# Block rows of the mask moved between a DMA, VectorE and GpSimd in a fused attention and gated MLP kernel

## The chip, the cores and the metric

The kernel runs on one core of a Trainium2 chip. The metric is the device time of one execution in microseconds (us). TensorE (PE, weight loads PEld), VectorE (DVE), ScalarE (ACT), GpSimd (POOL) and SyncE (SP, which here only issues DMAs) each work through a queue of their own in order and wait for one another by semaphores.

## The reference

Block-sparse attention (4 batches, 8 heads, 768 positions, head dimension 64), then a gated MLP with a product over positions. Inputs and output are float32.

```python
def _attn_ref(q, k, v, sampled_blocks):            # B, H, S, D = 4, 8, 768, 64
    scores = np.matmul(q, k.transpose(0, 1, 3, 2)) / np.sqrt(D)
    # blocks of 32: neighbours, first and last block row and column,
    # and 3 sampled key blocks for each query block
    scores = np.where(mask, scores, -1e9)
    attn = np.exp(scores - scores.max(-1, keepdims=True))
    attn = attn / (attn.sum(-1, keepdims=True) + 1e-09)
    return np.matmul(attn, v)

def _moe_ref(x, w_in, w_spatial, b_spatial, w_out):  # x: 4 x 768 x 512
    h = np.maximum(x @ w_in, 0.0)                     # 1024 wide
    u, v = h[..., :512], h[..., 512:]
    v_n = (v - mean(v)) / np.sqrt(var(v) + 1e-06)
    v_s = np.einsum('ts,bsd->btd', w_spatial, v_n) + b_spatial[None, :, None]
    return (u * v_s) @ w_out
```

## The kernel before

**The operand of the scores.** One tile `kq` of 88 partitions holds, for each of the 8 heads of a batch, the keys in its first 768 columns (`K_`) and the queries in the next 768. Partitions 0 to 63 hold the head dimension. Partitions 64 to 87 (`MR`) hold the mask, one partition for each of the 24 key blocks: a one-hot of the block in the key columns, and in the query columns what the mask adds to the scores of this block. One matmul over 88 rows so gives masked scores. The mask is the same for every head: it is made once, in head 0, and copied to the other heads. These copies are the block rows, and `rows` (L243) makes one on an engine, `rows_dma` (L250) by a DMA on the SP queue. Block rows are written once; later batches overwrite partitions 0 to 63 alone.

**Slots.** The program is a loop of slots (L845). Each slot puts the score matmuls of one piece into TensorE's queue, one exponential into ScalarE's queue, then the products with V of an earlier piece, then the work that tables assign to the slot, in this order: `at`, the MLP steps (`run_queue`), `late`, `post`. The order within each engine's queue is thus fixed when the program is built; the times follow from the waits.

Batch 0 takes the slots 0 to 35. Its queries come in three thirds of 256 columns (`qcols(0)`, `qcols(1)`, `qcols(2)`), and a unit (`UNITS`, L427) is one third for one pair of heads, three slots long:

| slots | what | block rows needed |
|---|---|---|
| 0 to 5 | first third (and more) of heads 0 and 1 | heads 0, 1 |
| 6 to 14 | first third of pairs 1, 2, 3 (pair 3, heads 6 and 7, in 12 to 14) | `K_` and `qcols(0)` of heads 2 to 7 |
| 15 to 23 | second third of pairs 1 to 3 | `qcols(1)` of heads 2 to 7 |
| 24 to 35 | third third of pairs 0 to 3 | `qcols(2)` of all heads |

From slot 36 on a head takes six slots, and the other three batches follow; their loads, casts, transposes (`tr_dma`) and copies into `kq` (`split`) are set by slot numbers (L816 to L829). The MLP products of batch 0 begin in slot 15 and run between the scores.

**Where block rows are made before the change.** VectorE copies most, by the list `ROWS` (L739): entries are slot, first head, last head, columns. `qcols(1)` of heads 2 and 3 and `qcols(2)` of heads 2 to 7 come by two DMAs (L332, L353).

**What stands around them.** In VectorE's queue: `tr_first` (L384) copies a pair's keys and first third from PSUM into `kq` in slots 4, 7 and 10 (pair 3 in 10); `normalize` (reciprocal L474, product L475 into `xn`); copies of transposed `xn` into `xt`; evictions of MLP products (`ts`, L186), the statistics of `v` (L619, L620) and its normalization, also L186, which waits for `rstd` from GpSimd (L625). In GpSimd's queue: float32 to bfloat16 casts of q, k, v (L137), of `w_in` (L234), of `w_spatial` (L556), in the order of the program. In the SP queue: the loads of batch 0 and of `w_in`, then `b_col` (L364), the loads of pair 4 (k, q, v), six loads `ws_f` of `w_spatial` and the transposing DMA of pair 4. A load waits for the buffer that it writes and for the DMA that was issued eight before it on this queue.

Of the kernel before, what the change touches and what calls it, by code (L numbers as in the profile page):

```python
# [26 lines left out]
def kernel(  # L27
# [16 lines left out]
    nc = tc.nc  # L44

    B, H, S, D = q.shape
    BLK = 32
    NB = S // BLK
# [16 lines left out]
    TW = TC * 128  # L65
# [17 lines left out]
    kq = const.tile([KR, H, 2 * S], BF16, name="kq")  # L83
    NVV = 6
    vv = [const.tile([128, 2, NCH, VS], BF16, name=f"vv{s}") for s in range(NVV)]
    MR = slice(D, KR)
    K_, Q_ = slice(0, S), slice(S, 2 * S)

    def qcols(t0, n=1):
        return slice(S + t0 * TW, S + (t0 + n) * TW)  # L90
# [24 lines left out]
    def nat0_view():  # L115
        return nat[0].rearrange("p c h d -> p (c h d)").rearrange("p (h x) -> p h x", h=2)

    def cast(p, nm, eng, hs=BOTH, cs=ALLC):
        if nm == "v":
            dst = vv[p % NVV][:, hs, cs, 0:D]  # L120
        else:
            if p not in nat:
                nat[p] = work.tile([128, 2 * NCH, 2, D], BF16, tag="nat", bufs=4, name="nat")
            c0 = 0 if nm == "k" else NCH
            dst = nat[p][:, c0 + cs.start:c0 + cs.stop].rearrange("p c h d -> p h c d")[:, hs]
        src = st[nm, p].rearrange("p h (c d) -> p h c d", d=D)[:, hs, cs]
        if p == 0 and nm != "v":
            dst = nat0_view()[:, hs, (c0 + cs.start) * D:(c0 + cs.stop) * D]
            if cs is not C45:
                dst = dst[:, 0].rearrange("p (i t d) -> p t i d", t=2, d=D)  # L130
                src = src[:, 0].rearrange("p (t i) d -> p t i d", t=2)
            else:
                dst = dst.rearrange("p h (c d) -> p h c d", d=D)
        if eng is nc.scalar:
            nc.scalar.activation(out=dst, in_=src, func=AF.Copy)
        else:
            eng.tensor_copy(out=dst, in_=src)  # L137
# [77 lines left out]
    PL, DV = nc.gpsimd, nc.vector  # L215
# [14 lines left out]
    def w_in_load(u, g):  # L230
        w_load((u, g), moe_w_in[g * 128:(g + 1) * 128, 0 if u else DH:DH if u else DFF])

    def w_in_cast(u, g, eng):
        eng.tensor_copy(out=w_in_t[:, g, 0 if u else DH:DH if u else DFF], in_=wst.pop((u, g)))  # L234
# [8 lines left out]
    def rows(hs, cs, eng=nc.vector):  # L243
        src = kq[MR, 0:1, cs].to_broadcast([NB, hs.stop - hs.start, cs.stop - cs.start])
        if eng is nc.scalar:
            nc.scalar.activation(out=kq[MR, hs, cs], in_=src, func=AF.Copy)
        else:
            eng.tensor_copy(out=kq[MR, hs, cs], in_=src)  # L248

    def rows_dma(t, h1):  # L250
        nc.sync.dma_start(out=kq[MR, 2:h1, qcols(t)],
                          in_=kq[MR, 0:1, qcols(t)].to_broadcast([NB, h1 - 2, TW]))

    cast(0, "k", nc.scalar, H0, C03)
    cast(0, "q", PL, H0, C03)
    rows(H1, K_)
# [72 lines left out]
    m1()  # L329
    m2()  # L330
    rows(H1, qcols(0, 3))
    rows_dma(1, 4)  # L332
    w_in_load(0, 1)
    load(2, "q", cs=C25)
    w_in_load(0, 2)
# [9 lines left out]
    cast(1, "v", PL)  # L345
    cast(2, "v", PL)
    cast(1, "q", PL, cs=C25)
    w_in_cast(0, 0, PL)
    w_in_load(1, 3)
    cast(3, "v", PL)  # L350
    w_in_cast(0, 1, PL)
    w_in_load(1, 2)
    rows_dma(2, H)  # L353
    cast(2, "q", PL, cs=C25)
    w_in_cast(0, 2, PL)
    w_in_cast(0, 3, PL)
# [376 lines left out]
    def when(slot, *fns):  # L733
        at.setdefault(slot, []).extend(fns)

    def c(f, *a, **kw):
        return lambda: f(*a, **kw)

    ROWS = [(1, 2, 4, qcols(0)), (1, 2, 3, K_), (3, 3, 4, K_), (4, 4, 6, qcols(0)), (6, 4, 6, K_), (7, 6, 8, qcols(0)), (9, 6, 8, K_), (15, 4, 8, qcols(1))]  # L739
    when(0, second)  # L740
    when(1, third)
    when(2, lambda: filler(FILL3, psum.tile([128, 512], FP32, tag=moe_tag(), bufs=1, name="wps")))
# [3 lines left out]
    when(10, c(tr_first, 3))  # L746
    for sl, h0, h1, cs in ROWS:
        when(sl, c(rows, slice(h0, h1), cs))
# [146 lines left out]
```

## Time and profile before

| | us |
|---|---|
| median of 3 runs | 211.81 |
| lowest, highest | 211.39, 212.13 |
| profiled execution, its own time | 212.83 |
| its span, first to last instruction | 209.9 |
| granted TensorE clock, mean | 0.997 |

The profile is of one execution. A line of a timeline gives start, duration, engine, source line, operation, output<-input and, in brackets, idle time of the engine before it and what ended it. SPq and PEq are sequencers; an SPq row is the issue of a DMA, not its transfer. A line of the chain of waits gives start, duration and the instruction that the end depended on. The engine groups of the page, the windows, the chain and the timelines that matter are shown in the prediction.

### The profile page before, as it was taken

To read this page: it belongs to the slowest core of one execution; us is meant where nothing else is said; L and a number is where in the kernel's file an instruction comes from. 1 tells how busy PE (TensorE), PEld (TensorE's weight loads), DVE (VectorE), ACT (ScalarE), POOL (GpSimd) and SP (SyncE) were. 2 spreads that over 40 slices of the span, in tenths; PEclk is the share of its full clock that TensorE was granted. 3 is DMA by queue.
4 is the path that set the end of the run, shared out by engine and by line. 5 is a ranking of instruction groups with operands and counts; after the bars stand their busy time and mean duration, and the time that the engine had idled before them with its cause. 6 is when DMAs were issued, how large, how long until landed. Compare 5 with 4: busy or idle time off the path is not lost.

```text
span 209.9 us, 5241 instructions
## 1 busy us (share of the span) xinstructions
PE 200.5 (96%) x2107; PEld 127.1 (61%) x2141; DVE 133.7 (64%) x294; ACT 167.7 (80%) x222; POOL 69.7 (33%) x108
## 2 busy tenths in 40 slices
PE   7898999899999999999999999999999999999992
PEld 6597878666666666665565556665565556544441
DVE  7899675988864545484986464375884443476551
ACT  5898999899989989989998888979999787266021
POOL 6685759675564123033065050131020000012000
PEclk9999999999999999999999999999999999999998
DMA  5999899999999999999955597795101225520275
GB/s 146 343 363 324 279 352 253 272 232 249 275 350 241 257 185 285 242 293 336 209 194 112 131 246 167 202 269 159 37 3 35 52 53 118 196 78 0 50 191 211
DMA packets 64356, 41.93 MB, mean 200 GB/s; under 512 B 45196, under 2 KB 59084, under 8 KB 64332
## 3 DMA queue, kind: packets, MB, share of 16 engines
q1 hardware_dynamic: 63756, 41.01, 75.7%
q10 hardware_dynamic: 576, 0.59, 0.8%
q8 instruction: 16, 0.26, 0.6%
q14 instruction: 8, 0.07, 0.1%
HBM read 24.38 MB, written 6.29 MB: 146 GB/s over the span
## 4 chain that ended last, share of the span: by engine, by line
PE 78%; DVE 6%; DMA 5%; POOL 3%; SPq 2%; issue 2%; ACT 1%; ACTq 0%; DVEq 0%
PE ps_moe L584 29%; PE ps L459 22%; PE ps_av L510 12%; PE ps_t L584 8%; PE ps_sc L584 4%; DMA ws_f<-in_moe_w_spatial_dram 3%; POOL ws_b L556 2%; DVE kq L218 2%; DMA st_q<-in_q_dram 2%; DVE vn L186 2%; SPq L109 2%; PE ps_av L492 1%; PE ps L446 1%; DVE kq L248 1%; PE ps L293 1%
## 5 line engine op out<-in xcount | busy, mean ns | idle before, releaser
L463 ACT ACTIVATE a_all<-ps 128x768 bf16<-128x768 f32 x144 | 113.6, 812 | 14.5 <-PE ps L459 8.2
L459 PE MATMUL ps<-kq 88*128 88x384 bf16 x288 | 70.4, 325 | 0.4
L510 PEld LDWEIGHTS <-a_all 128*128 128x128 bf16 x864 | 45.2, 97 | 20.0
L510 PE MATMUL ps_av<-vv,a_all 128*128 128x65 bf16 x864 | 49.8, 193 | 0.0
L459 PEld LDWEIGHTS <-kq 88*128 88x128 bf16 x288 | 27.7, 98 | 29.6
L584 PE MATMUL ps_moe<-w_in_t,xt 128*128 128x512 bf16 x127 | 38.6, 378 | 0.5
L451 ACT ACTIVATE a_all<-ps 128x1024 bf16<-128x1024 f32 x36 | 34.2, 1026 | 3.0 <-PE ps L446 2.7
L584 PE MATMUL ps_moe<-vn,w_spt 128*128 128x512 bf16 x99 | 30.2, 378 | 0.4
L137 POOL CAST nat<-st_k 128x768 bf16<-128x768 f32 (+2 forms) x17 | 13.2, 781 | 39.6 <-DMA st_k<-in_k_dram 38.0
L446 PE MATMUL ps<-kq 88*128 88x256 bf16 (+1 forms) x140 | 21.6, 275 | 2.0 <-ACT a_all L451 0.9
L656 DVE SCALAR_TENSOR_TENSOR un<-ps_moe,b_col,un 128x512 bf16<-128x512 f32 x18 | 13.4, 746 | 13.6 <-PE ps_moe L584 11.3
L623 POOL TENSOR_SCALAR std<-mv 128x3 f32<-128x3 f32 (+1 forms) x9 | 2.2, 240 | 58.2 <-DVE mv L620 41.1
L474 DVE RECIPROCAL rc<-ps_av 128x6 f32<-128x6 f32 (+1 forms) x36 | 6.6, 183 | 21.5 <-PE ps_av L510 20.0
L584 PEld LDWEIGHTS <-xt 128*128 128x128 bf16 x192 | 15.5, 98 | 7.6 <-DVE xt L218 0.2
L584 PE MATMUL ps_moe<-w_out_t,gt 128*128 128x512 bf16 x66 | 19.7, 378 | 0.2
L475 DVE TENSOR_TENSOR xn<-ps_av,rc 128x384 bf16<-128x384 f32 (+1 forms) x36 | 18.5, 513 | 1.2
L137 POOL CAST nat<-st_q 128x768 bf16<-128x768 f32 (+2 forms) x21 | 14.8, 706 | 8.5 <-DMA st_q<-in_q_dram 8.2
L619 DVE BATCH_NORM_STATS2 stats<-vn 128x6 f32<-128x512 bf16 x24 | 16.4, 684 | 1.3 <-ACT vn L614 0.9
L137 POOL CAST vv<-st_v 128x768 bf16<-128x768 f32 x16 | 13.8, 863 | 9.4 <-DMA st_v<-in_v_dram 9.0
L186 DVE TENSOR_SCALAR vn<-vn,mv,rstd 128x512 bf16<-128x512 bf16 x24 | 14.0, 615 | 4.4 <-POOL rstd L625 4.4
L218 DVE COPY kq<-tt 64x1536 bf16<-64x1536 bf16 x24 | 14.8, 618 | 2.9 <-DMA tt<-nat 2.6
L446 PEld LDWEIGHTS <-kq 88*128 88x128 bf16 x140 | 12.5, 97 | 5.8 <-DVE kq L218 1.9
(81 smaller groups left out, 202.5 us busy)
## 6 DMA issues: line engine op xcount, KB each, us to landing
st_v<-in_v_dram SPq DMA_DIRECT2D x16, 384.0 KB, 6.1
st_k<-in_k_dram SPq DMA_DIRECT2D x15, 384.0 KB, 4.5
out_dram<-osb SPq DMA_DIRECT2D x22, 256.0 KB, 3.1
st_q<-in_q_dram SPq DMA_DIRECT2D x12, 384.0 KB, 5.6
ws_f<-in_moe_w_spatial_dram SPq DMA_DIRECT2D x6, 384.0 KB, 7.6
w_f<-in_moe_w_in_dram SPq DMA_DIRECT2D x8, 256.0 KB, 5.5
w_f<-in_moe_w_out_dram SPq DMA_DIRECT2D x4, 256.0 KB, 4.0
st_q<-in_q_dram SPq DMA_DIRECT2D x6, 128.0 KB, 5.8
```

The source lines that it names most:

```text
L137: eng.tensor_copy(out=dst, in_=src)
L186: nc.vector.tensor_scalar(out=out, in0=in0, scalar1=s1, scalar2=s2, op0=o0, **kw)
L218: nc.vector.tensor_copy(out=o, in_=i)
L446: nc.tensor.matmul(out=ps[:, at:at + n * TW], lhsT=kq[:, h, ci * 128:(ci + 1) * 128], rhs=kq[:, h, qcols(t0, n)], start=True, stop=True)
L451: nc.scalar.activation(out=out, in_=ps, func=AF.Exp, scale=0.125)
L459: nc.tensor.matmul(out=ps[:, hf * 512:hf * 512 + HALF], lhsT=kq[:, j % H, ci * 128:(ci + 1) * 128], rhs=kq[:, j % H, S + hf * HALF:S + (hf ...
L463: nc.scalar.activation(out=a_ref["h", j][:, ci, :].rearrange("p (b c) -> p b c", b=2), in_=ps.rearrange("p (b c) -> p b c", b=2)[:, :, 0:H ...
L475: nc.vector.tensor_tensor(out=out, in0=ps[:, :, 0:D], in1=rc[:, 0:n].to_broadcast([128, n, D]), op=ALU.mult)
L510: nc.tensor.matmul(out=av_ref[j][:, qc, 0:VA], lhsT=a_ref["h", j][:, ci, qc * 128:(qc + 1) * 128], rhs=vv[p % NVV][:, h, ci, 0:VA], start= ...
L584: nc.tensor.matmul(out=ref["ps"][:, 0:w], lhsT=lhs(i), rhs=rhs(i), start=(i == 0), stop=(i == n - 1))
L619: nc.vector.bn_stats(out=stats, in_=self.vn[:, tcc, :])
L656: nc.vector.scalar_tensor_tensor(out=self.un[:, tcc, :], in0=ps, scalar=b_col[:, tcc:tcc + 1], in1=self.un[:, tcc, :], op0=ALU.add, op1=AL ...
```

## The change

Four edits. The DMA that copied `qcols(2)` to heads 2 to 7 is gone from the SP queue, and VectorE makes the same rows in slot 22. The rows `qcols(0)` of heads 6 and 7 are made by GpSimd, behind the cast of pair 1's later queries and ahead of the first `w_in` cast, and no longer by VectorE in slot 7. The rows `K_` of heads 6 and 7 move from slot 9 to slot 7, into the place that this leaves. The helper `rows_dma` is gone, and its other use is written out with the same operands.

```diff
@@ -246,10 +246,6 @@
-    def rows_dma(t, h1):
-        nc.sync.dma_start(out=kq[MR, 2:h1, qcols(t)],
-                          in_=kq[MR, 0:1, qcols(t)].to_broadcast([NB, h1 - 2, TW]))
@@ -329,7 +325,8 @@
     rows(H1, qcols(0, 3))
-    rows_dma(1, 4)
+    nc.sync.dma_start(out=kq[MR, 2:4, qcols(1)],
+                      in_=kq[MR, 0:1, qcols(1)].to_broadcast([NB, 2, TW]))
     w_in_load(0, 1)
@@ -345,12 +342,12 @@
     cast(1, "q", PL, cs=C25)
+    rows(slice(6, 8), qcols(0), PL)
     w_in_cast(0, 0, PL)
     w_in_load(1, 3)
     cast(3, "v", PL)
     w_in_cast(0, 1, PL)
     w_in_load(1, 2)
-    rows_dma(2, H)
     cast(2, "q", PL, cs=C25)
@@ -736,7 +733,7 @@
-    ROWS = [(1, 2, 4, qcols(0)), (1, 2, 3, K_), (3, 3, 4, K_), (4, 4, 6, qcols(0)), (6, 4, 6, K_), (7, 6, 8, qcols(0)), (9, 6, 8, K_), (15, 4, 8, qcols(1))]
+    ROWS = [(1, 2, 4, qcols(0)), (1, 2, 3, K_), (3, 3, 4, K_), (4, 4, 6, qcols(0)), (6, 4, 6, K_), (7, 6, 8, K_), (15, 4, 8, qcols(1)), (22, 2, 8, qcols(2))]
```

In the queues of the engines this is: VectorE has as many instructions as before (24 x 2 x 768 where 24 x 2 x 256 stood, the later 24 x 2 x 768 gone, one 24 x 6 x 256 behind the two copies of slot 21's `tr_rest`, ahead of an eviction of `vn`); GpSimd has one more (24 x 2 x 256), and TensorE's first scores of slot 12 wait for it; SP has one less. The order of TensorE's and ScalarE's queues is the same.

## The prediction

> **What bounds the kernel now.** I read the page first, then stages in the windows view, then the chain of waits in order of time, then the timelines of the engines where the chain leaves TensorE.
>
> ```profile
> span 209.9 us, 5241 instructions
> ...
> PE 200.5 (96%) x2107; PEld 127.1 (61%) x2141; DVE 133.7 (64%) x294; ACT 167.7 (80%) x222; POOL 69.7 (33%) x108
> ...
> 15.00:18.00 3.00, 2.17 (x32) 1.65 (x30) 2.83 (x7) 2.26 (x4) 0.89 (x3) 1.00 1.07 355
> ...
> 20.00:23.00 3.00, 2.95 (x49) 2.59 (x47) 2.55 (x8) 2.88 (x4) 2.71 (x5) 1.00 0.95 307
> 23.00:26.00 3.00, 2.92 (x46) 2.48 (x45) 1.64 (x6) 3.00 (x4) 1.74 (x5) 1.00 0.77 226
> 26.00:29.00 3.00, 3.00 (x43) 2.29 (x42) 2.09 (x5) 2.62 (x4) 2.03 (x3) 1.00 0.98 355
> ...
> 36.00:40.00 4.00, 3.43 (x39) 2.54 (x38) 3.24 (x5) 3.85 (x5) 3.09 (x3) 1.00 1.08 336
> ...
> 60.00:80.00 20.00, 19.79 (x226) 12.50 (x229) 10.52 (x22) 18.03 (x25) 7.61 (x10) 1.00 1.07 249
> ```
>
> The window columns are length, then busy time of PE, PEld, DVE, ACT and POOL, granted clock, DMA share, GB/s. From 60 us on TensorE is busy 19.79 of 20 us: what is won before is carried to the end as a shift. Two early stages are not full: 15 to 18 us (PE 2.17 of 3) and 36 to 40 (3.43 of 4). The chain of waits says who holds them up.
>
> ```profile
> 14.30 0.89 DVE kq L248
> ...
> 15.88 0.55 DVE kq L248
> 16.46 0.68 DVE kq L218
> ...
> 21.05 0.51 SPq L364
> ...
> 24.20 6.75 DMA ws_f<-in_moe_w_spatial_dram
> 31.00 4.60 POOL ws_b L556 x3
> 36.00 0.74 POOL rstd L625
> 36.76 1.65 DVE vn L186
> ```
>
> So there are two bounds one behind the other. Around 16 us it is VectorE's queue, two of whose pieces are block rows (L248). From 21 to 40 us it is the SP queue, then the loads behind it, GpSimd's casts of them, and VectorE's `vn` behind GpSimd. The change touches both.
>
> **First part: slots 7 to 12.** The scores of slot 12 (PE L446 at 17.20) wait for the `kq` copy at 16.46.
>
> ```profile
> 14.22 0.83 POOL L137 CAST vv<-st_v 128x768 bf16<-128x768 f32 x1 [0.23 <-DMA st_v<-in_v_dram]
> 15.00 0.67 POOL L137 CAST nat<-st_q 128x512 bf16<-128x512 f32 x1
> 17.78 0.62 POOL L234 CAST w_in_t<-w_f 128x512 bf16<-128x512 f32 x1 [2.11 <-DMA w_f<-in_moe_w_in_dram]
> ...
> 11.05 0.28 DVE L248 COPY kq<-kq 24x512 bf16<-24x512 bf16 x1
> ...
> 14.30 0.89 DVE L248 COPY kq<-kq 24x512 bf16<-24x512 bf16 x1
> ...
> 15.88 0.55 DVE L248 COPY kq<-kq 24x1536 bf16<-24x1536 bf16 x1
> 16.46 1.41 DVE L218 COPY kq<-ps 64x1024 bf16<-64x1024 bf16 x2
> ...
> 17.20 0.61 PE L446 MATMUL ps<-kq 88*128 88x256 bf16 x4 [0.71 <-ACT a_all L451]
> ...
> 17.91 9.59 ACT L451 ACTIVATE a_all<-ps 128x1024 bf16<-128x1024 f32 x10 [0.74 <-PE ps L446]
> ```
>
> The change takes one row copy out of VectorE's queue and puts the longer one where the shorter stood. The short form costs 0.28 us alone (11.05) but 0.89 at 14.30, where GpSimd's cast runs from 14.22 to 15.05: it ended at 15.20, just behind that cast. The long form costs 0.55 alone (15.88, GpSimd idle). Put at 14.30 it should end 0.55 - 0.28 = 0.27 later, at 15.47; reciprocal and `xn` follow 0.27 later too, and the copies, with no row copy ahead (15.88 to 16.46 is 0.58), start 0.58 - 0.27 = 0.31 earlier. I take **0.3 us**. Bounds: 0.74, the whole idle time of ScalarE there; and a loss of 0.34, if GpSimd's next cast (15.00) goes first: then the row copy ends near 15.67 + 0.45 = 16.12 (0.45 being 0.55 less some start-up, an estimate from the 0.28 and 0.55 rows), 0.92 after the old 15.20, of which the missing row copy gives back 0.58.
>
> [...]
>
> GpSimd's new copy (24 partitions x 512) has no row in the trace. Nearest below: a 128x256 cast (0.40, next fence); the 128x512 cast takes 0.62 (17.78); above, the strided `ws_b` cast, 4.60 / 3 = 1.53 for 768, thus 1.02 for 512. I take 0.62, its size. It starts when the cast of 15.00, pushed 0.27 by the longer row copy, is done: 15.94, and ends at 16.56, or 16.96 by the upper end. Slot 12's matmuls, which now wait for GpSimd as well (all of TensorE's later work queues behind them, and ScalarE's exponentials wait for it), get their keys at 16.46 - 0.31 + 0.68 = 16.83. VectorE's copy hides it with 0.27 to spare; the upper end costs 0.13. Behind it stands the `w_in` cast, idle until 17.78 for its load, so nothing on GpSimd gets late.
>
> **Second part: the SP queue.** The removed transfer and the loads behind it:
>
> ```profile
> 17.74 2.34 SPq L228 DMA_DIRECT2D w_f<-in_moe_w_in_dram  x4
> 20.18 0.82 SPq L251 DMA_DIRECT2D kq<-kq  x1
> 21.05 0.51 SPq L364 DMA_DIRECT2D b_col<-in_moe_b_spatial_dram  x1
> ...
> 25.47 0.40 POOL L137 CAST nat<-st_q 128x256 bf16<-128x256 f32 x1
> ...
> 26.37 0.83 POOL L137 CAST nat<-st_k 128x768 bf16<-128x768 f32 x1
> 27.92 0.83 POOL L137 CAST nat<-st_q 128x768 bf16<-128x768 f32 x1 [0.72 <-DMA st_q<-in_q_dram]
> 30.06 0.83 POOL L137 CAST vv<-st_v 128x768 bf16<-128x768 f32 x1 [1.31 <-DMA st_v<-in_v_dram]
> ```
>
> SP issues without a pause here, so `b_col`, pair 4's three loads and the six `ws_f` loads are issued 21.05 - 20.18 = 0.87 us earlier. Whether they land earlier depends on room in the DMA engines: the share is 0.95 in 20 to 23 and 0.77 in 23 to 26, against 0.98 to 1.08 around. The room is 3 x 0.05 + 3 x 0.23 = 0.84 us. GpSimd waits 0.72 and 1.31 for these loads, so its casts follow. I take **0.75 us**, between 0.69 (the emptier window alone) and 0.84; the ends are 0 (the engines fill nothing of it) and 0.87 (issue).
>
> **Third part: slot 22.** VectorE gets a copy of 24 x 1536 (0.55, above) behind the copies at 26.83, ahead of the eviction at 28.25.
>
> ```profile
> 26.83 0.58 DVE L218 COPY kq<-ps_av 64x256 bf16<-64x256 bf16 x2
> 28.25 0.69 DVE L186 TENSOR_SCALAR vn<-ps_moe 128x512 bf16<-128x512 f32 x1 [0.84 <-PE ps_moe L584]
> ...
> 29.06 0.60 PE L446 MATMUL ps<-kq 88*128 88x256 bf16 x4
> ```
>
> VectorE idles 0.84 there, which hides the 0.55, so nothing is charged. The first reader, slot 24's scores at 29.06 (28.76 with the 0.3), comes after it: 27.41 - 0.3 + 0.55 = 27.66. The cover goes if GpSimd's `st_q` cast, now 0.75 earlier at about 27.2, holds VectorE off: 0.83 later, 28.49, 0.54 after the eviction was due at 27.95. Queued behind are that eviction, the reciprocal and `xn`, and TensorE waits for the banks they free.
>
> **The sum.** At 40.10 two arms meet:
>
> ```profile
> 36.69 1.57 POOL L556 CAST ws_b<-ws_f 128x768 bf16<-128x768 f32 x1
> ...
> 40.10 0.65 PE L492 MATMUL ps_av<-vv,a_all 128*128 128x65 bf16 x16 [0.68 <-DVE xt L218]
> ```
>
> TensorE was ready at 40.10 - 0.68 = 39.42; with the first part at 39.12. The GpSimd-to-VectorE arm that it waits for comes at 40.10 - 0.75 = 39.35. The later sets it: 0.75 us earlier, the first part having only kept TensorE out of the way. Neither part alone would do: without the SP part the 0.3 drowns in the wait at 40.10; without the first part the gain would end at 0.68. The profiled execution took 212.83 us (span 209.9 and 2.9 around it), 1.02 over the median; the span becomes 209.15, the median 211.81 - 0.75 = **211.06**.
>
> [...]
>
> **Rivals.**
> 1. Larger (chance 0.06). GpSimd's cast no longer meets `vn`: the 1.65 shrinks. The arm drops below TensorE's 39.12, gain 0.98: **210.8**.
> 2. No gain (0.17). The loads land as before because the engines are full. For it: shares of 1.07 before 18 us. Against: 0.77 at 23 to 26. The arm stays at 40.10: **211.8**.
> 3. Slower (0.22). GpSimd gets in first wherever both stand ready. It decides at 15.00: the row copy ends after the cast of 15.00, near 16.1, not at 15.47. TensorE's arm then loses 0.34 there and 0.54 in slot 22: 39.42 + 0.88 = 40.30. The copies behind `vn` (itself already 1.65) then meet one cast of 0.83 more in 36 to 41; three quarters of it, 0.62, is counted, an estimate, since the wait can begin anywhere in the cast. Together 40.10 becomes 40.92: **212.6** (212.0 to 212.8 with none or all of that cast). Against it: the 0.89 row, where VectorE went first.
>
> **How the numbers follow.** The forecast has 0.55; its own range is 210.8 to 211.3 (0.5 to 0.98 gained). Over and under 0.3%, 0.64 us, which is about what a measurement of this kernel can tell, it splits 0.44 to 0.11. Of the slower rival 0.20 lies over 0.64, 0.02 under it. Faster: 0.44 + 0.06 = 0.50; within: 0.11 + 0.17 + 0.02 = 0.30; slower: 0.20. The range runs from a little under the larger gain to the slower rival: 210.6 to 212.6.
>
> **What would show it.** Right: ScalarE's idle time before slot 12 falls from 0.74 to about 0.45; the row copy in slot 7 lasts about 1.15; the new GpSimd copy ends before VectorE's first `kq` copy; `b_col` issues near 20.2; the share in 23 to 26 rises over 0.9; the `ws_b` casts begin near 30.25; TensorE's wait of 0.68 falls to about 0.2. Wrong: `ws_b` casts still at 31.0, TensorE waiting for GpSimd in slot 12, or a copy over 0.8 us in slot 22.

## The result and the profile after

The changed kernel took 210.22 us (median of 7 runs, 209.93 to 211.12) beside 211.81 for the kernel before (7 runs, 211.11 to 212.13): a ratio of 0.9934, 95% interval 0.9905 to 0.9963 (a ratio here is taken over the runs and is not the quotient of the two medians). That is faster, as forecast, but 0.84 us under the forecast of 211.06 and under the low end of the range, 210.6. Run twice more on other occasions, in 12 runs each (e6 on chip 9, e15 on chip 14; the chip of the first result is not on record), it gave 211.13 beside 211.63 (0.9968, 0.9942 to 0.9995) and 211.17 beside 211.44 (0.9977, 0.9946 to 1.0008). The three means lie 1.37, 0.57 and 0.39 us under those of the kernel before; weighted by the runs, (7 x 1.37 + 12 x 0.57 + 12 x 0.39) / 31 = **0.68 us** gained, close to the forecast of 0.75, though not for its reasons, as the last sections show. The first result looks like a favourable draw from runs that spread over 2.7 us (209.91 to 212.59 in these 31); a difference of the chips is not excluded. Two single runs further down, one of e4 and one of e7, were over 1.5% above the fastest of their kernel, and medians and ratios leave them out.

The page and the windows of the changed kernel's profile (its execution took 209.94 us), with the columns of before:

```profile
span 208.1 us, 5243 instructions
...
PE 200.8 (97%) x2107; PEld 127.5 (61%) x2141; DVE 132.3 (64%) x294; ACT 167.4 (80%) x222; POOL 71.0 (34%) x109
```

```profile
15.00:18.00 3.00, 2.90 (x44) 2.42 (x41) 2.73 (x7) 3.00 (x4) 1.74 (x3) 1.00 1.07 355
...
23.00:26.00 3.00, 2.92 (x51) 2.58 (x51) 1.81 (x6) 3.00 (x4) 2.25 (x5) 1.00 0.98 309
...
36.00:40.00 4.00, 3.95 (x58) 3.22 (x57) 3.93 (x9) 3.85 (x5) 2.90 (x4) 1.00 1.51 337
60.00:80.00 20.00, 19.84 (x229) 12.50 (x229) 9.88 (x19) 18.23 (x26) 6.09 (x9) 1.00 1.10 236
```

Both early gaps of TensorE are closed: 2.17 became 2.90 of 3 us at 15 to 18, 3.43 became 3.95 of 4 at 36 to 40. The DMA share in 23 to 26 rose from 0.77 to 0.98. Between 60 and 80 us TensorE is as full as before.

The first part, from the timelines of VectorE, GpSimd and ScalarE (start, duration, instruction, idle time before it):

```profile
14.73 0.55 DVE L248 COPY kq<-kq 24x1536 bf16<-24x1536 bf16 x1
...
16.05 1.41 DVE L218 COPY kq<-ps 64x1024 bf16<-64x1024 bf16 x2
...
14.79 0.97 POOL L137 CAST nat<-st_q 128x512 bf16<-128x512 f32 x1
15.82 0.61 POOL L248 COPY kq<-kq 24x512 bf16<-24x512 bf16 x1
...
14.74 12.37 ACT L448 ACTIVATE a_all<-ps 128x1024 bf16<-128x1024 f32 x13 [0.26 <-PE ps L443]
```

VectorE's key rows took 0.55 and GpSimd's cast beside them 0.97, where before the row copy had taken 0.89 beside a cast that took its usual 0.83 (14.22): this time VectorE came first. ScalarE runs 13 exponentials without a printed pause from 14.74 on, so the 0.74 before slot 12 is gone; 0.26 stands before slot 9 instead, where the kernel before had no pause.

The second part, from the timelines of SP, GpSimd, VectorE and TensorE:

```profile
19.97 0.42 SPq L361 DMA_DIRECT2D b_col<-in_moe_b_spatial_dram  x1
...
29.29 4.62 POOL L553 CAST ws_b<-ws_f 128x768 bf16<-128x768 f32 x3 [0.16 <-DMA ws_f<-in_moe_w_spatial_dram]
...
27.05 0.62 DVE L248 COPY kq<-kq 24x1536 bf16<-24x1536 bf16 x1
27.86 0.69 DVE L186 TENSOR_SCALAR vn<-ps_moe 128x512 bf16<-128x512 f32 x1 [0.19 <-PE ps_moe L581]
...
35.30 1.42 DVE L186 TENSOR_SCALAR vn<-vn,mv,rstd 128x512 bf16<-128x512 bf16 x1
...
38.88 0.65 PE L489 MATMUL ps_av<-vv,a_all 128*128 128x65 bf16 x16
```

`b_col` is issued 1.08 us earlier than in the profile of before (21.05), the casts of `ws_f` begin 1.71 earlier (31.00), and the matmuls that had waited 0.68 at 40.10 now start at 38.88 with no wait. The new copy of slot 22 lies in VectorE's former idle time, 0.84 before and 0.19 now.

### The profile page after: what moved, and what is told of

It reads as the page before. It is cut to its first block, busy times and chain, and to the rows that moved or that the text cites. A ratio compares the mean times of both kernels' runs of the same rounds, so it can differ in the third digit from the quotient of the medians.

```text
span 208.1 us, 5243 instructions
## 1 busy us (share of the span) xinstructions
PE 200.8 (97%) x2107; PEld 127.5 (61%) x2141; DVE 132.3 (64%) x294; ACT 167.4 (80%) x222; POOL 71.0 (34%) x109
## 4 chain that ended last, share of the span: by engine, by line
PE 89%; DVE 5%; ACT 2%; issue 2%; ACTq 0%
PE ps_moe L581 31%; PE ps L456 23%; PE ps_av L507 12%; PE ps_t L581 8%; PE ps L443 5%; PE ps_sc L581 4%; PE ps_av L489 3%; DVE kq L218 3%; PE wps L180 1%; DVE kq L248 1%; ACT a_all L448 1%; PE ps L289 1%; PE ps_av L289 1%; ACT osb L221 0%; ACT a_all L460 0%
## 5 line engine op out<-in xcount | busy, mean ns | idle before, releaser
L581 PEld LDWEIGHTS <-w_spt 128*128 128x128 bf16 x144 | 11.6, 98 | 5.6
```

The costliest lines, as they stand in the source:

```text
L581: nc.tensor.matmul(out=ref["ps"][:, 0:w], lhsT=lhs(i), rhs=rhs(i), start=(i == 0), stop=(i == n - 1))
```

## The experiments

Each kernel was timed in 12 runs (the late transfer in 6), beside 29 to 35 runs of the kernel before on the same chip. There were four batches on four chips: e1 to e4, e5 to e8, e9 to e12, e13 to e15. Times of different batches are compared by their ratios.

| | median, us | before | ratio (95% interval) |
|---|---|---|---|
| first part alone, e1 | 211.71 | 211.39 | 1.0021 (0.9994 to 1.0047) |
| first part alone, e10 | 211.75 | 211.21 | 1.0039 (1.0010 to 1.0067) |
| second part alone, e2 | 210.48 | 211.39 | 0.9961 (0.9937 to 0.9985) |
| second part alone, e9 | 211.10 | 211.21 | 0.9987 (0.9963 to 1.0012) |
| changed, transfer put back, e3 | 211.58 | 211.39 | 1.0012 (0.9987 to 1.0036) |
| changed, three transfers, e4 | 212.36 | 211.39 | 1.0076 (1.0046 to 1.0107) |
| kernel before again, e5 | 211.72 | 211.63 | 1.0009 (0.9984 to 1.0034) |
| changed again, e6 | 211.13 | 211.63 | 0.9968 (0.9942 to 0.9995) |
| changed, transfer late, e7 | 213.59 | 211.63 | 1.0099 (1.0060 to 1.0139) |
| changed, no row transfer at all, e8 | 211.06 | 211.63 | 0.9965 (0.9937 to 0.9993) |
| changed, more fillers, e11 | 211.88 | 211.21 | 1.0033 (1.0010 to 1.0057) |
| changed, fewer fillers, e12 | 211.30 | 211.21 | 0.9995 (0.9973 to 1.0017) |
| changed, issue without transfer, e13 | 211.59 | 211.44 | 1.0007 (0.9985 to 1.0030) |
| changed, transfer from GpSimd, e14 | 211.06 | 211.44 | 0.9985 (0.9963 to 1.0007) |
| changed a third time, e15 | 211.17 | 211.44 | 0.9977 (0.9946 to 1.0008) |

**Each part by itself.**

```diff
 # e1 and e10: the kernel before, and
+    rows(slice(6, 8), qcols(0), PL)        # behind cast(1, "q", PL, cs=C25)
-    ROWS: (7, 6, 8, qcols(0)), (9, 6, 8, K_)
+    ROWS: (7, 6, 8, K_)
 # e2 and e9: the kernel before, and
-    rows_dma(2, H)
+    ROWS: (22, 2, 8, qcols(2))
```

> The kernel before with the first part of the change alone: rows of heads 6 and 7 by GpSimd and their key rows in slot 7; the DMA of the third third stays on the SP queue, no copy in slot 22. Theory A (two waits one behind the other, the later arm sets the time at slot 35): ScalarE's wait before slot 12 shrinks from 0.74 us to under 0.2, but TensorE's wait near 40 us, 0.68 before, grows by as much, and the time stays within 0.3 us of the kernel before. Theory B (each part is worth its own): 0.75 us faster than before. Theory C (the SP queue is hidden anyway, the first part is all): 1.4 us faster.

> The kernel before with the other part alone: the DMA of the third third is gone from the SP queue and VectorE copies these rows in slot 22; rows of heads 6 and 7 as before. Theory A: the wait of 0.68 us near 40 us goes, the 0.74 us before slot 12 stays: 0.7 us faster than before. Theory B: 0.65 us faster, no telling from A by this run alone. Theory C: no change, within 0.2 us.

The first part alone gained nothing in e1 and lost 0.82 us in e10 (0.0039 of 211.21), a little more than was expected. The second alone gained 0.82 us (0.0039 of 211.39), then 0.27, which the interval does not tell from nothing. TensorE's wait near 40 us, which theory A wanted to see grow in e1, is in neither profile of the first part. The second profile of the first part shows what it costs, TensorE above and GpSimd below:

```profile
18.62 0.60 PE L447 MATMUL ps<-kq 88*128 88x256 bf16 x4 [0.27 <-POOL kq L248]
...
17.29 0.61 POOL L137 CAST nat<-st_q 128x512 bf16<-128x512 f32 x1 [1.42 <-DMA st_q<-in_q_dram]
17.97 0.61 POOL L248 COPY kq<-kq 24x512 bf16<-24x512 bf16 x1
```

GpSimd's copy is queued behind a cast that waits 1.42 us for a load. In this execution the load was late, and slot 12's scores waited for GpSimd: the new wait that the prediction named as the sign of being wrong. ScalarE idled 0.70 before slot 12 all the same. In the first profile slot 12 was well, and TensorE waited for GpSimd's casts ten slots later:

```profile
26.39 0.29 PE L306 MATMUL ps_av<-ident,nat 128*128 128x128 bf16 x2 [0.23 <-POOL nat L137]
```

> The second part alone once more. If it carries nearly the whole gain of the change, the ratio is again near 0.996 (0.8 us), within 0.3 us of the changed kernel's two results (0.9934 and 0.9968). If its first result was a favourable draw, it lies within 0.4 us of the kernel before, and the gain needs both parts. In the profile: the idle time before the exponential of slot 12 shows whether this wait (0.74 in both profiles of the kernel before, gone in the first profile of this kernel) is tied to the first part at all.

> The first part alone once more. Expected again no gain (ratio 0.998 to 1.003), although the wait of 0.74 before slot 12 is gone from its profile: it comes back later, as in the first profile, where TensorE waited for GpSimd's cast near 26 us and ScalarE idled 0.70 before 27.80. If that wait was a chance, the ratio should fall to 0.997 (0.6 us).

**The transfer put back, and tripled.** The two further transfers of e4 go to parts of the tiles `hot` and `lim` that nothing reads any more, half the size each.

```diff
 # e3: the changed kernel, and (VectorE's copy in slot 22 stays)
+    nc.sync.dma_start(out=kq[MR, 2:H, qcols(2)],
+                      in_=kq[MR, 0:1, qcols(2)].to_broadcast([NB, H - 2, TW]))
 # e4: behind it two more, 24 x 3 x 256 each, to hot and to lim
```

> The changed kernel with the DMA of the third third put back in its place on the SP queue; VectorE still copies the same rows again in slot 22. Theory A: loads, GpSimd's casts and VectorE's normalization of v come about 1 us later, of the 1.3 us by which VectorE's copy into xt is now ahead of TensorE (37.7 against 39.0 us): as fast as the changed kernel within 0.3 us, 1.1 to 1.4 us faster than before. Theory B: 0.65 us lost, 0.75 us faster than before. Theory C: as the changed kernel, 1.4 us faster than before.

> The changed kernel with three DMAs in that place: the one of the third third and two of half its size into tiles that are no longer read (they write there what nothing needs). Theory A: the arm over the SP queue is 2 to 2.6 us later, more than its lead of 1.3: the wait near 40 us comes back with 0.7 to 1.3 us, and the time is 0.1 to 0.7 us faster than before. Theory B: 0.65 us lost for each DMA of full size, about as before or 0.1 us faster. Theory C: 1.4 us faster than before, no wait near 40 us.

I had expected e3 to keep the gain in theory A, and it lost all of it; e4 lost 1.6 us against the kernel before, which no theory had it do. With none, one and three transfers at this place the ratios are 0.9934 to 0.9977, 1.0012 and 1.0076: the more issues, the slower. The profile of e4 shows three issues (19.47, 20.34 and 21.17) ahead of `b_col` at 22.00, and in a later place VectorE's normalization comes too late for TensorE:

```profile
51.45 0.38 PE L587 MATMUL ps_moe<-w_in_t,xt 128*128 128x512 bf16 x1 [1.05 <-DVE vn L186]
```

**Second looks at both kernels.**

> The kernel before, unchanged, as a second look at it. In the profile shown before the change the first exponential began at 5.58 us, and ScalarE idled 0.75 before the one at 41.55. Theory A (the arm of loads and casts is regularly later than TensorE at 40 us): the idle time there comes again, at least 0.4 us, and the ratio is 1.000 within its interval. Theory B (that wait was a chance of one execution): the idle time at 36 to 42 us is under 0.2 us in this profile, though the median stays. The first exponential may begin anywhere from 5.58 to 6.45 us; where it begins later, the matmuls before 10 us are slower than 0.61 us for four.

> The changed kernel, unchanged, on the chip and in the batch of the other runs. If the first part is worth something only together with the second, it is faster than the second part alone was (ratio 0.9961): 0.993 again, 1.4 to 1.6 us under the kernel before. If the first part is worth nothing in any company, the ratio is that of the second part alone, 0.996, 0.8 us.

> The changed kernel a third time, on the chip of the two others. Its two results differ (0.9934 and 0.9968); expected between, 0.995, and no idle time over 0.4 us before the exponentials of slots 12, 22 and 36 in the profile. If the wait that the kernel before shows at one of these places in each of its profiles comes here too, the second part doesn't remove it but only makes it rarer.

The timelines of ScalarE, TensorE, GpSimd in the second profile of the kernel before:

```profile
18.34 9.59 ACT L451 ACTIVATE a_all<-ps 128x1024 bf16<-128x1024 f32 x10 [0.74 <-PE ps L446]
...
39.70 0.65 PE L492 MATMUL ps_av<-vv,a_all 128*128 128x65 bf16 x16
...
30.19 4.60 POOL L556 CAST ws_b<-ws_f 128x768 bf16<-128x768 f32 x3
```

The 0.74 before slot 12 came again, to the hundredth. The wait at 40 did not: the same matmuls start at 39.70 without one, the `ws_f` casts beginning at 30.19 and not 31.00. So of the two bounds of the prediction the first came in both executions, and the second depends on the execution. The changed kernel was 0.68 us (0.0032 of 211.63) under the kernel before in e6 and 0.49 (0.0023 of 211.44) in e15.

**Where the transfer stands, and what it moves.** Three kernels take these apart. In e7 and e14 VectorE's copy in slot 22 is left out, since the transfer makes these rows.

```diff
 # e7: the transfer behind the six ws_f loads
+    when(19, lambda: nc.sync.dma_start(out=kq[MR, 2:H, qcols(2)], ...))
 # e13: its place in SP's queue without its bytes (rows of 64 bytes, to dead parts of tiles)
+    nc.sync.dma_start(out=hot[MR, 0, 0:32], in_=kq[MR, 0, S:S + 32])
+    nc.sync.dma_start(out=lim[MR, 0, 0:32], in_=kq[MR, 0, S:S + 32])
 # e14: its bytes without its place, behind GpSimd's new copy
+    nc.gpsimd.dma_start(out=kq[MR, 2:H, qcols(2)], ...)
```

> The changed kernel, but the rows of the third third come by the SP transfer again, issued behind the six ws_f loads; VectorE makes no copy in slot 22. Theory S (what counted was the transfer's place on SP ahead of the loads): as fast as the changed kernel, 1.4 us under the kernel before. Theory T (the transfer's packets take the DMA engines' time wherever it stands): no faster than the kernel before, ratio 0.998 to 1.003. Theory V (a wait for it at slot 27): it issues near 26.4 us and lands about 4.5 us later, near 31, and TensorE's scores of slot 27 begin near 32, so no wait; if there is one, ScalarE idles over 0.5 us near 32.6.

The late transfer could not decide it, since it met a wait of its own; SP, TensorE and ScalarE:

```profile
26.23 0.82 SPq L832 DMA_DIRECT2D kq<-kq  x1
...
34.27 0.61 PE L443 MATMUL ps<-kq 88*128 88x256 bf16 x4 [1.02 <-DMA kq<-kq]
...
34.98 1.94 ACT L448 ACTIVATE a_all<-ps 128x1024 bf16<-128x1024 f32 x2 [1.56 <-PE ps L443]
```

TensorE had it 8.0 us after its issue, not 4.5, with the six `ws_f` loads issued ahead of it (21.53 to 25.60), and slot 27, the first reader of these rows, waited 1.02 us.

> The changed kernel with two tiny transfers (24 rows of 64 bytes, into dead parts of tiles) on SP where the row transfer stood: they delay the issue of everything behind by 0.6 to 0.9 us and move almost nothing. Theory S (the place on SP): the gain is lost, ratio 0.999 to 1.002. Theory T (the 72 KB of small pieces occupy the DMA engines): as fast as the changed kernel, ratio 0.994 to 0.997.

> The changed kernel with the rows of the third third moved by the same transfer, but issued by GpSimd behind its new copy, so that SP's loads keep their early place; no copy in slot 22. Theory T: the gain is lost, ratio 0.999 to 1.003. Theory S: as fast as the changed kernel, 0.994 to 0.997, unless the issue on GpSimd (it idles 1.2 us there) delays its casts: then the profile shows GpSimd's queue late at 17.6 and at the casts of 25 to 31 us.

Theory T alone can't explain e13: two transfers of 24 x 64 bytes took the gain away (1.0007 beside the changed kernel's 0.9977 on the same chip; the two intervals overlap a little). The same 72 KB issued by GpSimd cost nothing that can be told (0.9985), but this lies between what the two theories forecast, and its interval reaches into both, so e14 decides nothing. The profile of e13 has the wait at 40 back; SP, GpSimd, TensorE, ScalarE:

```profile
20.15 0.79 SPq L351 DMA_DIRECT2D hot<-kq  x1
21.00 0.72 SPq L352 DMA_DIRECT2D lim<-kq  x1
21.77 0.51 SPq L363 DMA_DIRECT2D b_col<-in_moe_b_spatial_dram  x1
...
31.25 4.58 POOL L555 CAST ws_b<-ws_f 128x768 bf16<-128x768 f32 x3 [0.16 <-DMA ws_f<-in_moe_w_spatial_dram]
...
40.18 0.65 PE L491 MATMUL ps_av<-vv,a_all 128*128 128x65 bf16 x16 [0.84 <-DVE xt L218]
...
41.63 1.02 ACT L450 ACTIVATE a_all<-ps 128x1024 bf16<-128x1024 f32 x1 [0.91 <-PE ps L445]
```

The issue of `b_col` at 21.77 is 1.62 us behind the first tiny transfer's, twice what was expected and nearly twice the 0.87 of the row transfer, so e13 tests a longer delay than the one that the change removed. The casts start at 31.25, and the very matmuls of the first profile wait 0.84 us for VectorE's `xt` copy.

**One transfer fewer.** e8 lets GpSimd make the last transferred rows too (heads 2 and 3 of the second third), behind its new copy, and takes that transfer out.

> The changed kernel with the last row transfer (heads 2 and 3 of the second third, 0.97 us of issue at 11.07) taken out as well; GpSimd copies these 24x512 (0.61 us) behind its new copy, where it idled 1.20 us. Theory S or T (each transfer that goes brings the loads forward): 0.3 to 1.0 us under the changed kernel, near 209.5. Theory P (the arm is already under TensorE's own chain, which is 89% of the chain of waits after the change): as fast as the changed kernel within 0.3 us.

0.9965, as the changed kernel in the same batch (0.9968): theory P. No kernel run here beats the changed one.

**The start.** The first exponential began anywhere from 5.58 to 6.45 us, and in the kernels up to here late starts go with slow matmuls. e11 and e12 change the dummy matmuls on `warm` that run on TensorE ahead of the real work.

```diff
-    FILL, FILL2, FILL3 = 24, 4, 4
+    FILL, FILL2, FILL3 = 24, 12, 4     # e11
+    FILL, FILL2, FILL3 = 8, 4, 4       # e12
```

> The changed kernel with twelve filler matmuls instead of four between the first transposes (FILL2). Theory C (the spread of the times, 2 us from the fastest to the slowest run, is how long TensorE runs at half pace at the start: until 3.9 to 5 us in some profiles, until 10.2 in three of nine, told apart by the first exponential at 5.6 to 6.05 or at 6.45): fillers keep TensorE busy, the long half pace gets rarer, and the median falls by 0.2 to 0.8 us under the changed kernel's, the highest runs by over 1 us. If the half pace is not set by how busy TensorE is, the median rises by 0.1 to 0.5 us, the fillers' own time.

> The changed kernel with eight filler matmuls instead of 24 at the start (FILL). Theory C: TensorE leaves the half pace later, in nearly every run; the profile shows the first exponential at 6.45 us or later and four matmuls of 88x256 at over 1.0 us until about 10 us, and the median rises by 0.5 to 1.3 us over the changed kernel's. If the early pace is worth nothing at the end (later waits absorb it), the median stays within 0.3 us.

With fewer fillers the profile has the long half pace, the first exponential at 6.42, and the ratio is about 0.0035 over the mean of the changed kernel's three (0.9960), 0.7 us, as theory C has it, though those three come from other batches. More fillers cost the changed kernel's whole gain and more, but not by a half pace. In the one profile the matmuls run at full pace when the scores begin, and the first exponential is as late as 6.45 without it. From TensorE's timeline of e11:

```profile
5.81 0.60 PE L443 MATMUL ps<-kq 88*128 88x256 bf16 x4
...
206.61 0.61 PE L581 MATMUL ps_sc<-w_out_t,gt 128*128 128x256 bf16 x4 [1.74 <-DMA gt<-un]
```

The time went elsewhere: 0.56 us of waiting for a GpSimd cast at 27.26, and 1.74 near the end for a transposing DMA. Whether more fillers make the long half pace rarer, one profile can't say.

## Why the prediction was right, and where not

The profiles side by side, from the timelines: ScalarE's idle time before slot 12 (under 0.15 isn't printed: 0), start of the exponential of slot 22, start of the first `ws_b` cast, the second less the first (the lag of the arm), TensorE's wait at 40 us, and the end: from the start of ScalarE's last copy (L221, at 204 to 207 us) to the end of the span. The profiles of e7, e11 and e12 are left out: a late transfer and other fillers move their places.

| profile | first exponential | idle before slot 12 | slot 22 | `ws_b` cast | lag | wait at 40 | end |
|---|---|---|---|---|---|---|---|
| before | 5.58 | 0.74 | 27.79 | 31.00 | 3.21 | 0.68 | 3.90 |
| before, e5 | 5.85 | 0.74 | 28.23 | 30.19 | 1.96 | 0 | 3.90 |
| first alone, e1 | 6.05 | 0.17 | 27.80 | 29.53 | 1.73 | 0 | 3.93 |
| first alone, e10 | 6.45 | 0.70 | 29.20 | 30.99 | 1.79 | 0 | 3.91 |
| transfer back, e3 | 6.45 | 0 | 28.84 | 28.84 | 0.00 | 0 | 3.90 |
| three transfers, e4 | 6.45 | 0 | 28.47 | 31.36 | 2.89 | 0 | 3.95 |
| issue alone, e13 | 6.03 | 0.34 | 27.71 | 31.25 | 3.54 | 0.84 | 4.00 |
| changed | 6.03 | 0 | 27.40 | 29.29 | 1.89 | 0 | 3.41 |
| changed, e6 | 5.69 | 0.30 | 27.44 | 28.98 | 1.54 | 0 | 3.41 |
| changed, e15 | 6.44 | 0 | 28.78 | 28.90 | 0.12 | 0 | 3.40 |
| second alone, e2 | 6.03 | 0 | 27.94 | 30.12 | 2.18 | 0 | 3.44 |
| second alone, e9 | 6.45 | 0.56 | 28.99 | 28.06 | -0.93 | 0 | 3.48 |
| no transfer, e8 | 6.02 | 0 | 27.48 | 28.00 | 0.52 | 0 | 3.22 |
| from GpSimd, e14 | 5.83 | 0 | 27.90 | 29.50 | 1.60 | 0 | 3.96 |

**First part: the mechanism right, the price in time nothing.** Where the row copy met the cast again, it took what was forecast (about 1.15):

```profile
14.22 1.15 DVE L248 COPY kq<-kq 24x1536 bf16<-24x1536 bf16 x1
...
17.40 2.86 ACT L448 ACTIVATE a_all<-ps 128x1024 bf16<-128x1024 f32 x3 [0.30 <-PE ps L443]
```

These are rows of e6: 1.15, and 0.30 of idle time left before slot 12 where 0.45 was forecast. In the first profile VectorE came first, lost nothing, and all of the 0.74 went. In both executions the one that started first kept its time and the other took longer: the copy issued 0.06 ahead of the cast took 0.55 and the cast 0.97, where a cast of its size takes 0.61 (19.51); in e6 the cast that started 0.08 ahead (14.14) took 0.83, and the copy 1.15. Why the times grow, and whether they do wherever the two meet, no run shows. That the copy would go ahead of the cast of 15.00, on which the choice of the 0.3 over the loss rests, was my estimate; these two executions show the copy ending ahead of that cast (15.28 before 15.76, and 15.37 before 15.85). Over the table the idle time averages 0.15 in the ten profiles with the first part and 0.51 in the four without: 0.36 saved, 0.3 forecast. GpSimd's copy took 0.61, for 0.62. These profiles also differ in how they start, so this is no measurement of the part alone. And yet "neither part alone would do" holds for the first part only: alone it gained nothing or lost, and what it added to the second can't be told from nothing (mean gain over the kernel before of the same batch: changed kernel 0.68 us in 31 runs, second part alone 0.47 in 24). Where the idle time comes back is shown for single executions, GpSimd's copy behind a late load (e10) and its casts ten slots later (e1), not as a sum.

**Second part: the loads came earlier as forecast, but most of the gain stands elsewhere.** The loads were issued 1.08 us earlier (0.87 forecast), the empty stretch of the DMA engines filled as it should (0.98), and the arm moved by 1.71 between the two first profiles. That pair flatters it: over the five profiles with one transfer ahead of the loads (before, e5, e1, e10, e3) the lag of the arm averages 1.74, over the seven without (changed, e6, e15, e2, e9, e8, e14) 0.99. That the difference is 0.75 proves little, since the lags in each group spread over 3 us. e13 shows that issue time ahead of the loads is enough to bring the wait back; that bytes cost nothing is not shown.

**The step that failed is the sum**: "At 40.10 two arms meet", "The later sets it: 0.75 us earlier", and from there "the span becomes 209.15". It took one execution's wait at one place for all that the change does, and put nothing behind it. Between the two first profiles the span fell by 1.83 us (unrounded, 209.88 and 208.05), and the timelines say where. ScalarE, before and then after:

```profile
27.79 4.89 ACT L451 ACTIVATE a_all<-ps 128x1024 bf16<-128x1024 f32 x5 [0.29 <-PE ps L446]
...
42.48 4.50 ACT L463 ACTIVATE a_all<-ps 128x768 bf16<-128x768 f32 x6
...
205.98 0.38 ACT L221 ACTIVATE osb<-ps_t 128x256 f32<-128x256 f32 x1 [0.41 <-DVE osb L218]
```

```profile
27.40 4.88 ACT L448 ACTIVATE a_all<-ps 128x1024 bf16<-128x1024 f32 x5 [0.29 <-PE ps L443]
...
41.25 4.49 ACT L460 ACTIVATE a_all<-ps 128x768 bf16<-128x768 f32 x6
...
204.65 0.38 ACT L221 ACTIVATE osb<-ps_t 128x256 f32<-128x256 f32 x1 [0.41 <-DVE osb L218]
```

Slot 22 came 0.39 earlier, from there to slot 36 it took 13.85 and not 14.69 (0.84 less), from slot 36 to the last copy 0.10 less, and from the last copy to the end of the span 3.41 and not 3.90 (0.49 less). So 1.23 was gained at 42 us where 0.75 was forecast, because TensorE itself, and not the arm, set the time there; and 0.5 stands behind the last matmul, where the prediction has no term.

Over the table these two pieces behave differently. The stretch from slot 22 to slot 36 takes 13.85 in every row but the two with the wait at 40 (14.69 in before, 14.84 in e13). The wait stands only at lags of 3.21 and 3.54, and not at 2.89 or below; of the five profiles with one transfer ahead of the loads one has it, so it is worth about 0.84 / 5 = 0.2 us on the mean (an estimate from five profiles). The end, however, takes 3.90 to 4.00 in each of the eight profiles that have the transfer of the third third, on SP or on GpSimd, or others in its place, 3.40 to 3.48 in the five without it, and 3.22 in e8, which has one transfer less still. e3, where the transfer alone is put back, has 3.90 again and no wait at 40: about half of what it lost beside the changed kernel stands there. The two pieces together, 0.2 and 0.5, come to about the mean gain of 0.68; that the forecast's 0.75 is so near to it is luck. Why the end of the program is shorter with one transfer less is open. The fastest spans of all runs go with it: 208.1 in each of the three results of the changed kernel, 208.1 and 208.4 in e2 and e9; 208.5 among 128 runs of the kernel before, 208.6 in e3 and e14.

The start of the kernel adds a spread that the range left out. Where the first exponential began by 6.05 us, the spans are 208.9 to 209.9 with the transfer (before, e5, e1) and 207.9 to 209.1 without (changed, e6, e2, e8, e14); where it began at 6.44 or 6.45, they are 209.9 and 210.3 with (e3, e10) and 209.4 and 209.7 without (e15, e9): TensorE is then late itself and the arm's lag falls to 0.12 or less in three of four. Of the 7 runs of the first result 6 took under 210.5 us; of the 24 later ones 7 did. More early starts among the 7 would explain how 0.7 us became 1.59; the start is known for the profiled run alone, so this is not shown.

**The other points.** The copy of slot 22 was hidden, as forecast, and even where GpSimd held it up. Its first reader is slot 27 (heads 2 and 3), as the wait in e7 shows, and not slot 24, which reads heads 0 and 1 alone: an error of the prediction that cost nothing. The shift was carried on: of the 1.23 us at slot 36 nothing was lost up to the last copy (1.33 there), so no room in TensorE's later work absorbed it. Of the rivals, the larger gain came in the first result, by its mechanism (TensorE's own chain being the later arm) and by the end, which it does not name; "no gain" fell, as the loads did land earlier. The slower one came in part, and at no price that shows. In e6 the copy of slot 22 was issued 0.10 us behind the start of GpSimd's `st_q` cast and took 1.14 us, over the 0.8 that the prediction named as a sign of being wrong:

```profile
27.09 1.14 DVE L248 COPY kq<-kq 24x1536 bf16<-24x1536 bf16 x1
```

It took 1.13 in e8 and 1.39 in e9; the stretch from slot 22 to slot 36 is 13.85 in all three.

## What to carry to other kernels

A wait in one profile is a sample: before a sum is built on it, look whether the lag behind it is regular (0.74 twice) or falls now over its threshold, now under it (3.21 with a wait, 1.96 without), and give the range what the start of the kernel alone spreads. Follow a gain through to the end of the span: here half a microsecond of it stood behind the last matmul. A small transfer ahead of a chain of loads can cost time by its issue, even where it has next to no bytes: here two of 24 x 64 bytes held SP 0.79 and 0.72 us, and the wait at 40 us was back with 0.84 (e13). Work put on an engine behind an instruction that waits for a load inherits that wait, as GpSimd's copy did behind the cast that waited 1.42 us (e10).

## What the hardware showed that I had not expected

**Issue time did not follow the bytes.** SP was held 0.79 and 0.72 us by transfers of 24 x 64 bytes (e13) and 0.82 by one of 72 KB (20.18 in the profile of before).

**A long half pace at the start.** The same matmuls at the same place, from TensorE's timelines of e6 and, below, e15, which are the same kernel:

```profile
5.94 0.60 PE L443 MATMUL ps<-kq 88*128 88x256 bf16 x4 [0.23 <-DVE kq L218]
```

```profile
6.31 1.06 PE L443 MATMUL ps<-kq 88*128 88x256 bf16 x4
...
9.03 1.03 PE L443 MATMUL ps<-kq 88*128 88x256 bf16 x4
...
10.22 0.49 PE L443 MATMUL ps<-kq 88*128 88x256 bf16 x3
```

And e15 in the windows view:

```profile
5.00:10.00 5.00, 5.00 (x30) 3.37 (x29) 4.10 (x11) 3.43 (x5) 2.68 (x11) 1.00 1.01 349
```

In e15 TensorE keeps half pace until about 10 us, though it is busy 5.00 of 5 us in that window and the granted clock stands at 1.00 there; so that column does not show it, and the durations do (1.06 and 0.60 for the same four matmuls). From one execution of the same kernel to the next it differs by over 4 us: full pace stands at 5.94 us in e6 and only at 10.22 in e15. What sets the pace, and why a busy stretch of 5 us passes without a rise, the rows here do not show.
